# Query spread, maximum broadcast and row split in a cached-attention kernel

## The chip, the core and the metric

The kernel runs on one core of a Trainium2 chip. A core has TensorE (PE in the profile), VectorE (DVE), ScalarE (ACT), GpSimd (POOL) and SyncE (SP), which work side by side and wait for each other with semaphores, an on-chip memory of 128 partitions (SBUF), an accumulator memory that TensorE writes (PSUM), and 16 DMA engines that bring data from HBM. The metric is the device time of one execution in microseconds; the median of three runs is given.

## The reference

One decoding step of a block in which attention over a cache and a gated feed-forward network are mixed by a gate. There are 4 batches, 32 heads, 4096 cached positions and 128 numbers a head, all float32:

```python
q = (x @ wq).reshape(B, 1, 32, 128)            # x: (4, 1, 512)
scores = einsum("bhqd,bhkd->bhqk", q, k_cache) * 128 ** -0.5
p = softmax(scores)
a = (p @ v_cache).reshape(B, 1, 4096) @ wo
b = (gelu(x @ w_gate) * (x @ w_up)) @ w_down   # 512 -> 1792 -> 512
g = sigmoid((x * gate_w).sum(-1, keepdims=True))
return g * a + (1 - g) * b
```

The two caches are 268 MB each, and every number of them is used once. wq and wo are 8.4 MB each, the three FFN weights 3.7 MB each.

## The kernel before, in words

**Tiles and loads.** A tile is one batch and two heads (HT = 2); there are NT = 64 tiles, and four tiles (one pair of heads, all batches) form a group g. Partition p of a tile belongs to head p // 64 and holds R = 64 positions of 128 numbers, so K and V of a tile are 4 MB each, 32 KB a partition. All big loads share a ring of NB = 5 buffers of that size (pool kv) and are issued in one order by SyncE: two of wq, k0, k1, v0, k2, v1 and so on, the gate and up weights behind v19 and v20 (FFN_AT = 20), k62 and k63 together ahead of v61, and w_down last, in four transfers of which the last is half as big. V of tile 63 comes in two halves. A load is issued when the buffer five loads earlier in that order is free. wo comes in eight transfers of 1 MB in a buffer of its own, one for two groups.

**Scores.** VectorE multiplies K by the query, which has to stand on all partitions of its head (`QB[g]`, made by `q_spread`), and sums each row of 128. `MOST` splits the 64 rows of a tile for the first 62 tiles: three pieces "D" of 20 rows that VectorE both multiplies and sums, and one piece "A" of 4 rows whose products ScalarE sums, with one activation a row (`sums`, L201 to L207). `LAST` splits the last two tiles (NL = 2), in which ScalarE sums 24 of the 64 rows; "U" is a second such piece in a buffer u of its own.

**Softmax.** `max_a` takes the maximum of each partition and transposes it to one row in PSUM. `soft_max` reduces that row to a maximum for each head (m2), sends it to the 64 partitions of its head with two small matmuls against ones (L233), scales it on ScalarE (nb) and takes two exponentials, whose sums are the denominators. The result lands in PM, in columns so that a matmul of 32 columns puts each head and batch in a row of its own.

**P times V and after.** `pv` accumulates 16 matmuls a tile over a group in PO; the profile lists two records for each of them. `gather` adds the four position classes of a group to 8 rows of 128 numbers (batch and head) and the denominators. `weigh` divides (ri, on) and, for each head and each of four 32-number pieces, multiplies by a column pattern `hsel` that repeats each batch eight times and picks the head: 8 matmuls a group, which put the transposed result in OT. `project_a` copies OT and multiplies by wo, 16 matmuls for two groups, into a_acc.

**Order.** Every engine runs its instructions in the order in which the program issues them. In tile i: the first product of tile i, then `soft_max(i - 1)`, in every fourth tile `weigh`, then the other products and sums of tile i, `pv(i - 1)`, `max_a(i)`, in some tiles `project_a`, the next `load_wo` and `q_spread` of the next group. After the loop stand pv of the last tile, the four parts of `ffn_down` (each waits for its transfer of w_down), and between them gather, weigh and project_a of the last group; then ta, res and the store.

Of the kernel before, what the change touches and what calls it, by code (L numbers as in the profile page):

```python
# [9 lines left out]
F32 = mybir.dt.float32  # L10
AF = mybir.ActivationFunctionType
OP = mybir.AluOpType
AX = mybir.AxisListType
# [4 lines left out]
def tile_gated_mix(ctx: ExitStack, tc: tile.TileContext, x, kc, vc, wq, wo, w_gate, w_up, w_down, gate_w, out):  # L18
    nc = tc.nc
    P = 128  # L20
    B, H, S, D = kc.shape
    DM = x.shape[2]
    F = w_gate.shape[1]
    KC = DM // P
    C4 = DM // 4
    HT = 2
    PH = P // HT
# [3 lines left out]
    TW = R * D  # L31
    RJ = 4

    MOST = (("A", 60, 64), ("D", 0, 20), ("D", 20, 40), ("D", 40, 60))
    LAST = (("U", 48, 56), ("A", 60, 64), ("D", 0, 20), ("U", 40, 48), ("A", 56, 60), ("D", 20, 40))
    NL = 2
    FFN_AT = 20
# [4 lines left out]
    consts = ctx.enter_context(tc.tile_pool(name="consts", bufs=1))  # L42
    kv = ctx.enter_context(tc.tile_pool(name="kv", bufs=NB))
    work = ctx.enter_context(tc.tile_pool(name="work", bufs=2))
# [35 lines left out]
    def load_next():  # L80
        n = next(loads, None)
        if n:
            load(*n)
# [5 lines left out]
        nc.sync.dma_start(WO[w], wo[w * 4 * D:(w + 1) * 4 * D, :].rearrange("(p e) n -> p e n", e=4))  # L89

    load_next()
    x_sb = consts.tile([B, DM], F32)
    nc.sync.dma_start(x_sb, x.rearrange("b s d -> (b s) d"))
    load_next()
    for _ in range(NB - 2):
# [4 lines left out]
    ident = consts.tile([P, P], F32)  # L100
    make_identity(nc, ident)
    ones = consts.tile([P, P], F32)
# [3 lines left out]
    for j in range(RJ):  # L106
        nc.vector.tensor_reduce(sel[:, j], ident.rearrange("p (c b m) -> p b m c", c=4, b=B)[:, :, HT * j:HT * (j + 1), :],
                                axis=AX.X, op=OP.add)

    hsel = consts.tile([B * HT, HT, B, 8], F32)  # L110
    for h in range(HT):
        nc.vector.tensor_copy(hsel[:, h], ident[:B * HT, h:B * HT:HT][:, :, None].to_broadcast([B * HT, B, 8]))


    PZ = 32 - RJ * HT
# [32 lines left out]
    for c in range(KC):  # L148
        w = T["q", c // 2].rearrange("p (c n) -> p c n", c=2)[:, c % 2, :]
# [7 lines left out]
    QT = consts.tile([P, 4, HG, B], F32)  # L157
    for s in range(2):
        ps = ps1.tile([P, HB, P], F32, name="q")
# [5 lines left out]
    QT = QT.rearrange("p j a b -> p (j a) b")  # L165
# [5 lines left out]

    def q_spread(g):
        ps = ps1.tile([P, B, D], F32, name="q")
        for b in range(B):
            for h in range(HT):
                nc.tensor.matmul(ps[h * PH:(h + 1) * PH, b, :], QT[:, HT * g + h, b:b + 1].to_broadcast([P, PH]),  # L176
                                 ident, start=True, stop=True)
        QB[g] = work.tile([P, B, D], F32, name="qb")
        nc.scalar.activation(QB[g], ps, AF.Copy)  # L179

# [5 lines left out]
    def parts(i):  # L186
        return LAST if i >= NT - NL else MOST

# [38 lines left out]
    def soft_max(i):  # L227
        g, b = divmod(i, B)
        m2 = work.tile([1, HT], F32, name="m2")
        nc.vector.tensor_reduce(m2, MT[i].rearrange("o (h p) -> o h p", h=HT), axis=AX.X, op=OP.max)  # L230
        nbp = ps2.tile([P, 1], F32, name="sm")
        for h in range(HT):
            nc.tensor.matmul(nbp[h * PH:(h + 1) * PH, :], ones[:1, :PH], m2[:, h:h + 1], start=True, stop=True)  # L233
        nb = work.tile([P, 1], F32, name="nb")
        nc.scalar.activation(nb, nbp, AF.Copy, scale=-scale)  # L235
        for h in range(HT):
            s = slice(h * PH, (h + 1) * PH)
            nc.scalar.activation(PM[i % 2][:, PZ:].rearrange("p (c m) -> p c m", m=32)[s, :, h:RJ * HT:HT],  # L238
                                 SC[i][s, :].rearrange("p (c j) -> p c j", j=RJ), AF.Exp, bias=nb[s, :], scale=scale,
                                 accum_out=RS[g % 2][s, b, h:h + 1])  # L240
# [6 lines left out]
    def project(acc, t, w, start, stop):  # L247
        for c in range(4):
            nc.tensor.matmul(acc[32 * c:32 * c + 32, :], t, w[:, c * C4:(c + 1) * C4], start=start, stop=stop)  # L249
# [11 lines left out]
    OS, OT = {}, {}  # L261
# [8 lines left out]
        nc.tensor.matmul(OS[g][:, D:], RS[g % 2].rearrange("p b h -> p (b h)"), ones[:, :1], start=True, stop=True)  # L270


    def weigh(g):
        ri = work.tile([B * HT, 1], F32, name="ri")
        nc.vector.reciprocal(ri, OS[g][:, D:])
        on = work.tile([B * HT, 4, D // 4], F32, name="on")
        nc.vector.tensor_scalar(on, OS[g][:, :D].rearrange("p (k e) -> p e k", e=4), ri, None, op0=OP.mult)  # L277
        w, r = divmod(g, 2)
        if r == 0:
            OT[w] = ps1.tile([P, 4, 32], F32, name="oT")  # L280
        for h in range(HT):
            q = 32 * (HT * r + h)
            for e in range(4):
                nc.tensor.matmul(OT[w][q:q + 32, e, :], on[:, e, :], hsel[:, h].rearrange("p b k -> p (b k)"),
                                 start=True, stop=True)

    def project_a(w):
        ot = work.tile([P, 4, 32], F32, name="ot")
        nc.scalar.activation(ot, OT[w], AF.Copy)
        for e in range(4):  # L290
            project(a_acc, ot[:, e, :], WO[w][:, e, :], (w, e) == (0, 0), (w, e) == (H // 4 - 1, 3))
# [34 lines left out]
    def ffn_down(j):  # L326
        w = T["d", 0].rearrange("p (f n) -> p f n", n=DM)
        for f in range(j * FG // P, min((j + 1) * FG, F) // P):
            project(b_acc, hT[:, f, :], w[:, f, :], f == 0, f == F // P - 1)


    q_spread(0)
    for i in range(NT):
        g, b = divmod(i, B)
        pair = i > B and i % B == 1
        first = scores_a(i)
        if 0 < i < NT - 1:
            soft_max(i - 1)
        if pair:
            weigh(g - 1)  # L340
        scores(i, first)
        load_next()
        if i == NT - 2:
            max_a(i)
            soft_max(i)
        if i == NT - 1:
            pv(i - 1, 0, 4)
            max_a(i)
            pv(i - 1, 4, 8)
            soft_max(i)  # L350
            pv(i - 1, 8)
        elif i > 0:
            pv(i - 1)
            load_next()
            if b == 0:
                gather(g - 1)
# [10 lines left out]
        if i + B < NT and b == 1:  # L367
            q_spread(g + 1)
# [7 lines left out]
    gather(H // HT - 1)  # L376
    ffn_down(1)
    weigh(H // HT - 1)
    ffn_down(2)
    project_a(H // 4 - 1)  # L380
    ta = consts.tile([P, C4], F32)
    nc.vector.tensor_scalar(ta, a_acc, g_cols[:, 0:1], None, op0=OP.mult)
    ffn_down(3)
    res = work.tile([P, C4], F32, name="res")
    nc.vector.scalar_tensor_tensor(res, b_acc, g_cols[:, 1:2], ta, op0=OP.mult, op1=OP.add)
    nc.sync.dma_start(out.rearrange("b s (c n) -> c (b s) n", c=4), res[::8])

# [21 lines left out]
```

## Time and profile before

| | us |
|---|---|
| median of 3 runs (1323.89 to 1324.14) | 1323.95 |
| the profiled execution | 1324.15 |
| its span, first to last instruction | 1322.4 |
| VectorE busy | 1157.2 |
| TensorE busy (matmuls) | 498.6 |
| ScalarE busy | 210.4 |
| GpSimd busy | 0.7 |

The page gives, in turn: the busy time of each engine; the span in 40 slices with the busy share of each engine in tenths, the share of time in which the DMA engines move data and their rate; the DMA queues; the chain of work that ended last, by engine; the costliest groups of instructions (line, engine, operation, out<-in, shape, count, then total busy us and mean ns, then the engine's idle time just before them and what ended most of it); and the transfers with the median time from issue to landing. A view of windows gives the busy time of PE, PE's weight loads, VectorE, ScalarE and GpSimd in a stretch, then the granted TensorE clock, the DMA share and GB/s. A timeline row is the start in us, the duration, engine, line, operation, and in brackets the idle time before it with its releaser. Matmul times are modelled, and the granted clock was 0.659 on average here.

### The profile page before, as it was taken

To read this page: it belongs to the slowest core of one execution; us is meant where nothing else is said; L and a number is where in the kernel's file an instruction comes from. 1 tells how busy PE (TensorE), PEld (TensorE's weight loads), DVE (VectorE), ACT (ScalarE), POOL (GpSimd) and SP (SyncE) were. 2 spreads that over 40 slices of the span, in tenths; PEclk is the share of its full clock that TensorE was granted. 3 is DMA by queue.
4 is the path that set the end of the run, shared out by engine and by line. 5 is a ranking of instruction groups with operands and counts; after the bars stand their busy time and mean duration, and the time that the engine had idled before them with its cause. 6 is when DMAs were issued, how large, how long until landed. Compare 5 with 4: busy or idle time off the path is not lost.

```text
span 1322.4 us, 9351 instructions
## 1 busy us (share of the span) xinstructions
PE 498.6 (38%) x3562; PEld 177.8 (13%) x3562; DVE 1157.2 (88%) x645; ACT 210.4 (16%) x963; POOL 0.7 (0%) x6
## 2 busy tenths in 40 slices
PE   3242433342442453433344243352433343253316
PEld 1011111111110110111111011110101111011102
DVE  1999899989899579998999989899899989999894
ACT  0111111101111111101101101101101101111133
POOL 0000000000000000000000000000000000000000
PEclk9566667666775775766766665766766665666668
DMA  9999999999999999999999999999999999999997
GB/s 411 430 427 429 434 433 431 428 429 433 432 432 429 430 433 431 431 427 433 431 434 432 429 432 431 431 430 431 433 429 431 431 434 431 428 431 430 436 430 315
DMA packets 21096, 565.28 MB, mean 427 GB/s; under 512 B 2472, under 2 KB 2488, under 8 KB 2620
## 3 DMA queue, kind: packets, MB, share of 16 engines
q1 hardware_dynamic: 21052, 564.69, 99.4%
q8 instruction: 28, 0.46, 0.1%
q14 instruction: 16, 0.13, 0.0%
HBM read 564.67 MB, written 0.01 MB: 427 GB/s over the span
## 4 chain that ended last, share of the span: by engine, by line
DMA 71%; DVE 24%; PE 4%; issue 0%; SPq 0%; ACT 0%; DVEq 0%
DMA kv<-in_A_k_cache 51%; DMA kv<-in_A_v_cache 18%; DVE pr L197 13%; DVE sc L204 9%; PE po L256 3%; DMA kv<-in_B_w_down 3%; DVE pa L197 1%; DVE m L230 0%; SPq L59 0%; DVE u L197 0%; PE sm L135 0%; PE b_acc L249 0%; PE q L322 0%; DVE m L223 0%; DVE on L277 0%
## 5 line engine op out<-in xcount | busy, mean ns | idle before, releaser
L256 PE MATMUL po<-kv,pm 128*32 128x512 f32 x2048 | 368.3, 884 | 493.9 <-DMA kv<-in_A_v_cache 488.4
L204 DVE TENSOR_REDUCE sc<-pr 128x20 f32<-128x2560 f32 x190 | 535.8, 2820 | 6.5
L197 DVE TENSOR_TENSOR pr<-kv,qb 128x2560 f32<-128x2560 f32 x190 | 535.3, 2817 | 4.2
L256 PEld LDWEIGHTS po<-kv,pm 128*32 128x32 f32 x2048 | 91.7, 155 | 715.4 <-issue 704.2
L197 DVE TENSOR_TENSOR pa<-kv,qb 128x512 f32<-128x512 f32 x66 | 45.6, 690 | 90.9 <-DMA kv<-in_A_k_cache 90.9
L235 ACT ACTIVATE nb<-sm 128x1 f32<-128x1 f32 x64 | 10.9, 170 | 574.2 <-PE sm L233 574.1
L225 PE MATMUL sm<-ident,m 128*1 128x128 f32 x64 | 19.2, 299 | 199.3 <-DVE m L223 199.3
L207 ACT ACTIVATE dump<-pa 128x128 f32<-128x128 f32 x264 | 81.7, 309 | 10.5 <-DVE pa L197 2.6
L233 PE MATMUL sm<-m,ones 1*64 1x1 f32 x256 | 22.4, 238 | 88.6 <-DVE m L230 88.6
L179 ACT ACTIVATE qb<-q 128x512 f32<-128x512 f32 x16 | 9.6, 597 | 261.1 <-PE q L176 261.1
L207 ACT ACTIVATION_READ_ACCUMULATOR dump<-pa 128x1 f32 x264 | 49.2, 186 | 0.0
L238 ACT ACTIVATE pm<-sc,nb 64x64 f32<-64x64 f32 x128 | 44.6, 348 | 3.0 <-ACT nb L235 0.2
L265 ACT ACTIVATE o<-po 128x512 f32<-128x512 f32 x16 | 9.6, 597 | 194.0 <-PE po L256 194.0
L225 PEld LDWEIGHTS sm<-ident,m 128*1 128x1 f32 x64 | 5.1, 79 | 243.3 <-issue 211.1
L233 PEld LDWEIGHTS sm<-m,ones 1*64 1x64 f32 x256 | 17.0, 182 | 106.4 <-DVE m L230 98.9
L176 PE MATMUL q<-ident,QT 128*64 128x128 f32 x256 | 27.2, 381 | 0.6 <-DVE QT L163 0.6
L238 ACT ACTIVATION_READ_ACCUMULATOR pm<-sc,nb 64x1 f32 x128 | 23.6, 185 | 0.0
L176 PEld LDWEIGHTS q<-ident,QT 128*64 128x64 f32 x256 | 21.5, 194 | 4.4 <-issue 3.0
L268 PE MATMUL sm<-o,sel 128*8 128x128 f32 x128 | 16.6, 273 | 10.7 <-ACT o L265 10.7
L223 DVE TENSOR_REDUCE m<-sc 128x1 f32<-128x64 f32 x64 | 14.1, 220 | 6.6
L230 DVE TENSOR_REDUCE m<-sm 1x2 f32<-1x128 f32 x64 | 17.4, 272 | 1.1 <-PE sm L225 1.1
L268 PEld LDWEIGHTS sm<-o,sel 128*8 128x8 f32 x128 | 10.3, 89 | 26.8 <-ACT o L265 24.9
(56 smaller groups left out, 129.3 us busy)
## 6 DMA issues: line engine op xcount, KB each, us to landing
kv<-in_A_k_cache SPq DMA_DIRECT2D x64, 4096.0 KB, 42.6
kv<-in_A_v_cache SPq DMA_DIRECT2D x63, 4096.0 KB, 34.0
kv<-in_A_wq SPq DMA_DIRECT2D x2, 4096.0 KB, 16.6
wo_sb<-in_A_wo SPq DMA_DIRECT2D x8, 1024.0 KB, 40.7
kv<-in_A_v_cache SPq DMA_DIRECT2D x2, 2048.0 KB, 39.7
kv<-in_B_w_gate SPq DMA_DIRECT2D x1, 3584.0 KB, 44.1
kv<-in_B_w_up SPq DMA_DIRECT2D x1, 3584.0 KB
kv<-in_B_w_down SPq DMA_DIRECT2D x3, 1024.0 KB, 30.4
```

The source lines that it names most:

```text
L176: nc.tensor.matmul(ps[h * PH:(h + 1) * PH, b, :], QT[:, HT * g + h, b:b + 1].to_broadcast([P, PH]), ident, start=True, stop=True)
L197: nc.vector.tensor_tensor(t, T["k", i].rearrange("p (r d) -> p r d", d=D)[:, r0:r1], QB[g][:, b:b + 1, :].to_broadcast([P, n, D]), op=OP.mult)
L204: nc.vector.tensor_reduce(SC[i][:, r0:r1], t, axis=AX.X, op=OP.add)
L207: nc.scalar.activation(dump, t[:, r - r0, :], AF.Copy, accum_out=SC[i][:, r:r + 1])
L223: nc.vector.tensor_reduce(m1, SC[i], axis=AX.X, op=OP.max)
L225: nc.tensor.transpose(MT[i], m1, ident)
L230: nc.vector.tensor_reduce(m2, MT[i].rearrange("o (h p) -> o h p", h=HT), axis=AX.X, op=OP.max)
L233: nc.tensor.matmul(nbp[h * PH:(h + 1) * PH, :], ones[:1, :PH], m2[:, h:h + 1], start=True, stop=True)
L235: nc.scalar.activation(nb, nbp, AF.Copy, scale=-scale)
L238: nc.scalar.activation(PM[i % 2][:, PZ:].rearrange("p (c m) -> p c m", m=32)[s, :, h:RJ * HT:HT], SC[i][s, :].rearrange("p (c j) -> p c j" ...
L256: nc.tensor.matmul(PO[g % 2][32 * c:32 * c + 32].rearrange("p j d -> p (j d)"), PM[i % 2][:, m0:m0 + 32], T["v", i][:, j * N:(j + 1) * N], ...
L268: nc.tensor.matmul(OS[g][:, :D], sel[:, j].rearrange("p b h -> p (b h)"), o[:, j, :], start=j == 0, stop=j == RJ - 1)
```

## The change

Five things are changed. (1) `q_spread`: GpSimd copies the query columns of a group to qx, each number repeated over the 64 columns of its head, and TensorE transposes the four batches: 4 transposes instead of 8 matmuls against a broadcast operand. qx has one buffer, which x used at the start. (2) `soft_max`: GpSimd copies the two maxima to a row of 128 (mb), and one transpose puts it on the partitions, instead of two matmuls. (3) `weigh`: VectorE makes a version of the divided rows for each head, with zeros for the other, so that 4 matmuls of 64 columns do what 8 of 32 did; hsel becomes small and bsel is new. (4) `MOST`: VectorE multiplies and sums all 64 rows in three pieces of 22, 21 and 21; ScalarE's piece is left in the last two tiles only. (5) In the tail, `project_a` of the last groups is issued ahead of `ffn_down(2)` instead of behind it. The tiles on and res have one buffer instead of two.

```diff
--- before.py
+++ after.py
@@ -31,7 +31,7 @@
     TW = R * D
     RJ = 4
 
-    MOST = (("A", 60, 64), ("D", 0, 20), ("D", 20, 40), ("D", 40, 60))
+    MOST = (("D", 0, 22), ("D", 22, 43), ("D", 43, 64))
     LAST = (("U", 48, 56), ("A", 60, 64), ("D", 0, 20), ("U", 40, 48), ("A", 56, 60), ("D", 20, 40))
     NL = 2
     FFN_AT = 20
@@ -89,7 +89,7 @@
         nc.sync.dma_start(WO[w], wo[w * 4 * D:(w + 1) * 4 * D, :].rearrange("(p e) n -> p e n", e=4))
 
     load_next()
-    x_sb = consts.tile([B, DM], F32)
+    x_sb = work.tile([B, DM], F32, name="qx", bufs=1)
     nc.sync.dma_start(x_sb, x.rearrange("b s d -> (b s) d"))
     load_next()
     for _ in range(NB - 2):
@@ -107,9 +107,11 @@
         nc.vector.tensor_reduce(sel[:, j], ident.rearrange("p (c b m) -> p b m c", c=4, b=B)[:, :, HT * j:HT * (j + 1), :],
                                 axis=AX.X, op=OP.add)
 
-    hsel = consts.tile([B * HT, HT, B, 8], F32)
-    for h in range(HT):
-        nc.vector.tensor_copy(hsel[:, h], ident[:B * HT, h:B * HT:HT][:, :, None].to_broadcast([B * HT, B, 8]))
+    hsel = consts.tile([B * HT, HT], F32)
+    nc.vector.tensor_reduce(hsel, ident[:B * HT, :B * HT].rearrange("p (b h) -> p h b", h=HT), axis=AX.X, op=OP.add)
+    bsel = consts.tile([B * HT, B, 8], F32)
+    nc.vector.tensor_copy(bsel, ident[:B * HT, 0:B * HT:HT][:, :, None].to_broadcast([B * HT, B, 8]))
+    nc.vector.tensor_tensor(bsel, bsel, ident[:B * HT, 1:B * HT:HT][:, :, None].to_broadcast([B * HT, B, 8]), op=OP.add)
 
 
     PZ = 32 - RJ * HT
@@ -171,10 +173,11 @@
 
     def q_spread(g):
         ps = ps1.tile([P, B, D], F32, name="q")
+        qx = work.tile([P, B, HT, PH], F32, name="qx", bufs=1)
+        nc.gpsimd.tensor_copy(qx, QT[:, HT * g:HT * g + HT, :].rearrange("p h b -> p b h")[:, :, :, None]
+                              .to_broadcast([P, B, HT, PH]))
         for b in range(B):
-            for h in range(HT):
-                nc.tensor.matmul(ps[h * PH:(h + 1) * PH, b, :], QT[:, HT * g + h, b:b + 1].to_broadcast([P, PH]),
-                                 ident, start=True, stop=True)
+            nc.tensor.transpose(ps[:, b, :], qx[:, b].rearrange("p h k -> p (h k)"), ident)
         QB[g] = work.tile([P, B, D], F32, name="qb")
         nc.scalar.activation(QB[g], ps, AF.Copy)
 
@@ -228,9 +231,10 @@
         g, b = divmod(i, B)
         m2 = work.tile([1, HT], F32, name="m2")
         nc.vector.tensor_reduce(m2, MT[i].rearrange("o (h p) -> o h p", h=HT), axis=AX.X, op=OP.max)
+        mb = work.tile([1, HT, PH], F32, name="mb", bufs=1)
+        nc.gpsimd.tensor_copy(mb, m2[:, :, None].to_broadcast([1, HT, PH]))
         nbp = ps2.tile([P, 1], F32, name="sm")
-        for h in range(HT):
-            nc.tensor.matmul(nbp[h * PH:(h + 1) * PH, :], ones[:1, :PH], m2[:, h:h + 1], start=True, stop=True)
+        nc.tensor.transpose(nbp, mb.rearrange("o h k -> o (h k)"), ident[:1, :1])
         nb = work.tile([P, 1], F32, name="nb")
         nc.scalar.activation(nb, nbp, AF.Copy, scale=-scale)
         for h in range(HT):
@@ -270,19 +274,22 @@
         nc.tensor.matmul(OS[g][:, D:], RS[g % 2].rearrange("p b h -> p (b h)"), ones[:, :1], start=True, stop=True)
 
 
+
     def weigh(g):
         ri = work.tile([B * HT, 1], F32, name="ri")
         nc.vector.reciprocal(ri, OS[g][:, D:])
-        on = work.tile([B * HT, 4, D // 4], F32, name="on")
-        nc.vector.tensor_scalar(on, OS[g][:, :D].rearrange("p (k e) -> p e k", e=4), ri, None, op0=OP.mult)
+        rh = work.tile([B * HT, HT], F32, name="rh")
+        nc.vector.tensor_scalar(rh, hsel, ri, None, op0=OP.mult)
+        on = work.tile([B * HT, 4, HT, D // 4], F32, name="on", bufs=1)
+        for h in range(HT):
+            nc.vector.tensor_scalar(on[:, :, h, :], OS[g][:, :D].rearrange("p (k e) -> p e k", e=4), rh[:, h:h + 1], None,
+                                    op0=OP.mult)
         w, r = divmod(g, 2)
         if r == 0:
             OT[w] = ps1.tile([P, 4, 32], F32, name="oT")
-        for h in range(HT):
-            q = 32 * (HT * r + h)
-            for e in range(4):
-                nc.tensor.matmul(OT[w][q:q + 32, e, :], on[:, e, :], hsel[:, h].rearrange("p b k -> p (b k)"),
-                                 start=True, stop=True)
+        for e in range(4):
+            nc.tensor.matmul(OT[w][64 * r:64 * r + 64, e, :], on[:, e].rearrange("p h k -> p (h k)"),
+                             bsel.rearrange("p b k -> p (b k)"), start=True, stop=True)
 
     def project_a(w):
         ot = work.tile([P, 4, 32], F32, name="ot")
@@ -376,12 +383,12 @@
     gather(H // HT - 1)
     ffn_down(1)
     weigh(H // HT - 1)
+    project_a(H // 4 - 1)
     ffn_down(2)
-    project_a(H // 4 - 1)
     ta = consts.tile([P, C4], F32)
     nc.vector.tensor_scalar(ta, a_acc, g_cols[:, 0:1], None, op0=OP.mult)
     ffn_down(3)
-    res = work.tile([P, C4], F32, name="res")
+    res = work.tile([P, C4], F32, name="res", bufs=1)
     nc.vector.scalar_tensor_tensor(res, b_acc, g_cols[:, 1:2], ta, op0=OP.mult, op1=OP.add)
     nc.sync.dma_start(out.rearrange("b s (c n) -> c (b s) n", c=4), res[::8])
```

## The prediction

> **What bounds the kernel now.** I read the page first: the busy sums, the tenths, the DMA queues and the chain that ended last.
>
> ```profile
> PE 498.6 (38%) x3562; PEld 177.8 (13%) x3562; DVE 1157.2 (88%) x645; ACT 210.4 (16%) x963; POOL 0.7 (0%) x6
> DMA  9999999999999999999999999999999999999997
> GB/s 411 430 427 429 434 433 431 428 429 433 432 432 429 430 433 431 431 427 433 431 434 432 429 432 431 431 430 431 433 429 431 431 434 431 428 431 430 436 430 315
> q8 instruction: 28, 0.46, 0.1%
> q14 instruction: 16, 0.13, 0.0%
> DMA 71%; DVE 24%; PE 4%; issue 0%; SPq 0%; ACT 0%; DVEq 0%
> kv<-in_A_k_cache SPq DMA_DIRECT2D x64, 4096.0 KB, 42.6
> kv<-in_A_v_cache SPq DMA_DIRECT2D x63, 4096.0 KB, 34.0
> ```
>
> The 16 DMA engines are full from the first slice to the last but one, at 427 to 436 GB/s. DVE's 88% is the tempting wrong reading, so I asked what DVE waits for, and then cut the span into stages.
>
> ```profile
> L197 DVE TENSOR_TENSOR pa<-kv,qb 128x512 f32<-128x512 f32 x66 | 45.6, 690 | 90.9 <-DMA kv<-in_A_k_cache 90.9
> L256 PE MATMUL po<-kv,pm 128*32 128x512 f32 x2048 | 368.3, 884 | 493.9 <-DMA kv<-in_A_v_cache 488.4 <-ACT dump L207 2.9 <-ACT pm L238 2.6
> 34.00:1300.00 1266.00, 470.51 (x3239) 165.83 (x3239) 1149.43 (x615) 204.61 (x949) 0.00 (x0) 0.65 1.00 431
> 1310.00:1315.00 5.00, 3.98 (x86) 2.63 (x78) 0.49 (x2) 0.60 (x1) 0.00 (x0) 1.00 0.71 296
> 1315.00:1318.00 3.00, 2.11 (x76) 1.86 (x72) 0.00 (x0) 0.28 (x1) 0.00 (x0) 1.00 0.31 119
> ```
>
> Both consumers end their waits on a landing: the first product of a tile on K (90.9 us), P times V on V (488.4 us). In the last row's columns, DMA share and GB/s close each line: 1.00 and 431 over 1266 us. So one 4 MB transfer takes 4.194 MB / 431 GB/s = 9.73 us, and the kernel is 565 MB at that rate plus a head and a tail. Compute matters only if it empties the DMA queue or lengthens the tail.
>
> How far from empty is it? From issue to landing a K transfer takes 42.6 us and a V 34.0 us (medians), of which its own movement is 9.73: some 33 and 24 us of work stand ahead of each at its issue. The tightest stretch is the start, where DVE still works off its backlog:
>
> ```profile
> 32.49 0.69 DVE pa L197
> 101.82 0.33 SPq L59
> 102.25 40.94 DMA kv<-in_A_k_cache
> 143.20 0.69 DVE pa L197
> ```
>
> The K issued at 102.25 landed 40.94 later, so 31.2 us were ahead of it; the V issued just before, at 101.82, had 31.2 - 9.7 + 0.4 = 21.9 us ahead. That is the lead: a buffer must come free some **20 us later** than now before the chip's DMA pauses.
>
> **The change, part by part.**
>
> *All 64 rows on VectorE.* Gone are one product of 4 rows and ScalarE's 4 sums a tile; the three pairs grow from 20 to 22, 21 and 21 rows.
>
> ```profile
> L204 DVE TENSOR_REDUCE sc<-pr 128x20 f32<-128x2560 f32 x190 | 535.8, 2820 | 6.5
> L197 DVE TENSOR_TENSOR pr<-kv,qb 128x2560 f32<-128x2560 f32 x190 | 535.3, 2817 | 4.2
> L223 DVE TENSOR_REDUCE m<-sc 128x1 f32<-128x64 f32 x64 | 14.1, 220 | 6.6
> L230 DVE TENSOR_REDUCE m<-sm 1x2 f32<-1x128 f32 x64 | 17.4, 272 | 1.1 <-PE sm L225 1.1
> L277 DVE TENSOR_SCALAR on<-sm,ri 8x128 f32<-8x128 f32 x16 | 5.4, 339 | 0.6
> ```
>
> Products of 512 and 2560 elements (690 and 2817 ns) give (2817 - 690) / 2048 = 1.04 ns an element and 0.16 us fixed. So 22 rows take 3.08 us and 21 rows 2.95; a tile's products and sums go from 3 x (2.82 + 2.82) + 0.69 = 17.60 to 2 x (3.08 + 2.95 + 2.95) = 17.97 us. With both maxima (0.22 + 0.27) that is 18.09 before and 18.46 after. weigh() adds one tiny multiply (about 0.15, as other tiny ones) and a second 0.34 per four tiles: from 0.12 to 0.24 us a tile, so 18.70 in all. The DMA period of a tile is 2 x 9.73 = 19.46, and with 1 MB of wo every eighth tile 19.77. VectorE stays **1.07 us a tile** inside it. Its total rises by 62 x 0.37 + 16 x 0.49 = 31 us to about 1188; cost 0. The cover is the landing wait of the pa row; were it gone, each tenth of a microsecond over would cost 62 x 0.1 = 6 us.
>
> In the backlog phase, six tiles from 32.49 to 143.20, K buffers come free up to 6 x 0.4 = 2.4 us later: 19.5 us of lead are left. The first product now takes 3.08 instead of 0.69, and the maximum of the tile before (L230) stands behind it, so softmax and P times V can start 2.4 us later. V lands 9.73 us after K, which hides it; where it doesn't, V buffers go back 2 to 3 us later, against more than 20. ScalarE loses 62 x 4 sums: it is at 16% and releases nothing on the chain, so nothing.
>
> *Maxima and queries through GpSimd.* No row shows such a copy. The nearest:
>
> ```profile
> masks.py:199 POOL TENSOR_SCALAR_AFFINE_SELECT ident<-ident 128x128 f32<-128x128 f32 x1 | 0.3, 292 | 0.1
> L398 POOL MEMSET const-float32-0.0<- 128x1 f32 x1 | 0.1, 98 | 0.2 <-issue 0.2
> 29.99 0.60 ACT L179 ACTIVATE qb<-q 128x512 f32<-128x512 f32 x1 [2.89 <-PE q L176]
> ```
>
> One element takes 98 ns, 128 take 292: 1.5 ns each. So mb (128 elements) takes 0.3 us and qx (512) 0.9; the low ends are 0.1, the high ends 5 us (held up behind three products, below). I take 0.3 and 0.9. In the loop both stand ahead of P times V and are hidden like the 2.4 us above. At the head, qb is ready at 30.59 and K lands at 32.49: 1.9 us of cover. Behind a late mb wait PE's next transpose, weigh's matmuls and P times V; then the V buffer, with its 20 us of lead.
>
> *TensorE.* A matmul has two records, a transpose one (L225: 64 transposes, 64 records).
>
> ```profile
> L176 PE MATMUL q<-ident,QT 128*64 128x128 f32 x256 | 27.2, 381 | 0.6 <-DVE QT L163 0.6
> L233 PE MATMUL sm<-m,ones 1*64 1x1 f32 x256 | 22.4, 238 | 88.6 <-DVE m L230 88.6
> L284 PE MATMUL oT<-hsel,on 8*32 8x32 f32 x256 | 11.4, 213 | 2.1 <-DVE on L277 1.7
> ```
>
> These become 64, 64 and 128 records: 512 fewer, and as many weight loads. Busy PE was never the bound: 0. But instructions are themselves fetched over the 16 engines (the two instruction queues, 0.59 MB). With 1024 fewer on PE, 496 on ACT, some 44 on DVE and 80 more on POOL, 16% of the 9351 go, about 0.09 MB. Spread evenly at 431 GB/s that is 0.2 us; all on the engine that ends last (431 / 16 = 27 GB/s), 3.5 us. The engines do end unevenly: the two tail windows leave 5 x 0.29 + 3 x 0.69 = 3.5 us idle on average before the last one is through. I take **-0.6**, nearer to the even share, and keep -0.2 to -3.5.
>
> *The tail.*
>
> ```profile
> 1314.13 1.08 PE L249 MATMUL b_acc<-kv,hT 128*32 128x128 f32 x32 [0.49 <-DMA kv<-in_B_w_down]
> 1315.76 0.28 ACT L289 ACTIVATE ot<-oT 128x128 f32<-128x128 f32 x1 [3.94 <-PE oT L284]
> 1316.62 1.08 PE L249 MATMUL b_acc<-kv,hT 128*32 128x128 f32 x32 [0.89 <-DMA kv<-in_B_w_down]
> 1317.51 1.06 PE L249 MATMUL a_acc<-wo_sb,ot 128*32 128x128 f32 x32
> 1318.39 0.62 PE L249 MATMUL b_acc<-kv,hT 128*32 128x128 f32 x16
> 1319.11 0.35 DVE L385 SCALAR_TENSOR_TENSOR res<-b_acc,g_cols,ta 128x128 f32<-128x128 f32 x1
> ```
>
> The second and third piece of w_down land 2.49 us apart (1314.13 and 1316.62); the fourth is half as big, so it is there at about 1317.87, while its matmuls start at 1318.39 because project_a stands before them. Moved ahead of ffn_down(2), project_a runs in the wait before 1316.62 (ot is ready at 1316.04), and the last matmuls start with their data: **-0.5** (0 if ot comes 0.5 us later; weigh's extra 0.5 us on DVE is hidden behind ffn_down(1)).
>
> Sum on the profiled execution (1324.15, span 1322.4, 1.75 around it): -0.6 - 0.5 = -1.1, 1323.05. That execution lies 0.2 above the median 1323.95, so the forecast is **1322.9**.
>
> **The rivals.** *A: the tail's GpSimd copies are locked out.* In the last two tiles the order after a maximum is product, product, product:
>
> ```profile
> 1286.01 0.28 DVE L230 TENSOR_REDUCE m<-sm 1x2 f32<-1x128 f32 x1 [0.56 <-PE sm L225]
> 1286.22 1.20 DVE L197 TENSOR_TENSOR u<-kv,qb 128x1024 f32<-128x1024 f32 x1
> 1287.95 2.80 DVE L197 TENSOR_TENSOR pr<-kv,qb 128x2560 f32<-128x2560 f32 x1
> 1293.53 1.21 DVE L197 TENSOR_TENSOR u<-kv,qb 128x1024 f32<-128x1024 f32 x1
> 1301.03 0.22 DVE L223 TENSOR_REDUCE m<-sc 128x1 f32<-128x64 f32 x1
> 1311.22 0.60 ACT L265 ACTIVATE o<-po 128x512 f32<-128x512 f32 x1 [6.14 <-PE po L256]
> ```
>
> If a copy can't read SBUF while DVE multiplies, mb waits from 1286.2 to 1290.8. ScalarE's exponentials and its 24 sums of tile 63 queue behind it, so u and pa are read 4.6 us later than now; the second u product, at 1293.53, has some 1.6 us to spare, and the maximum at 1301.03 comes about 3 us later. Tile 62 has the same order, so 6 us together: 1307. From there the path has softmax (3 us, copy included) and P times V (32 records of 0.11 to 0.21 us by the clock, 3.4 to 6.8 us), which ends at 1313.5 to 1317 instead of 1311.2. From that point to the end of res it is 8.3 us today (to 1319.46), 1.5 of them waits for w_down that would be gone: res ends at 1320.3 to 1323.8, against 1318.95 in the forecast. Price +1.4 to +4.8, so 1324.3 to 1327.7, middle 1326. Against it: one product may let the copy in (then 0). In all other tiles a sum of 3 us follows the maximum, and the copy fits beside it. The Trainium skill states such a lock (SBUF — State Buffer, Who interferes with whom): a VectorE instruction with two SBUF inputs and a GpSimd one that reads SBUF exclude each other for a whole instruction. No run here shows it yet.
>
> *B: transfers get slower by their place in SBUF.* x and hsel leave the constants (2048 + 96 bytes a partition, tiles rounded to 32), so all kv buffers move down by 2144 = 8 x 256 + 96 bytes. For: 1 MB of w_down, in rows a quarter as long, takes 2.49 us where 431 GB/s gives 2.43: 0.06 us for 6 more rows on each engine (128 rows over 16 engines make 8 a transfer, where 1 MB of K would have 2), 10 ns each, so a row has a fixed cost. With 8 rows an engine in 9.73 us that is 0.8% of the transfer, some 10 us of 1266; if a worse start adds between a quarter and all of it, 2.5 to 10 us, middle 6.3: 1329.2. Against: nothing in this trace varies the start. The Trainium skill (DMA: Bandwidth & Descriptors, How a descriptor splits into AXI transactions) lets a descriptor that starts off a 256-byte boundary pay for the bytes below its start; no run here shows that for a write.
>
> *C: VectorE becomes the bound.* If GpSimd's reads hold up products by 1.5 us a tile, 0.43 x 62 = 27 us less the 20 of lead: 1330. The copies last 0.3 us, so unlikely.
>
> *D: the fetches saved sit on the last engine.* -3.5 instead of -0.6: 1320.0. For: the 3.5 us of uneven end. Against: one engine would have to carry all of them.
>
> **How the numbers follow.** Forecast 0.66, A 0.13, B 0.08, C 0.05, D 0.08. A measurement here tells 0.2% from no change, 2.65 us: faster is under 1321.3, slower over 1326.6. Faster: most of D and 0.02 of the forecast's spread, 0.09. Slower: B, C and half of A, 0.20. Same: 0.71. The range 1320.5 to 1328.5 leaves out B, C, A's top and D's bottom, 0.18; the forecast's own range is 1321.5 to 1324.0.
>
> **What would show it.** Right: DMA share 1.00 and 431 GB/s over the middle, DVE busy near 1188 us with its idle time still ended by K landings, POOL copies near 0.3 and 0.9 us, issue-to-landing times within 3 us of 42.6 and 34.0, the last b_acc matmuls ended by w_down's landing, fewer instruction bytes. Wrong: under 429 GB/s in the middle (B), products that last over 3.1 us or idle time on GpSimd (C), or a tail in which the last maximum comes over 2 us later against the last landing (A).

## The result, and the profile after

| | us | runs |
|---|---|---|
| before | 1324.05 (1323.86 to 1324.16) | 11 |
| after | 1327.21 (1326.58 to 1328.34) | 11 |
| ratio after / before | 1.0024, 95% interval 1.0015 to 1.0034 | |

The change costs 3.2 us, just over the 2.65 us that the prediction called no change. The forecast of 1322.9 is missed by 4.3 us; the time lies inside the range, where rival A put it (1324.3 to 1327.7).

First the page of the changed kernel: busy sums, tenths of the DMA share, GB/s, the two instruction queues, the chain that ended last, and issue to landing.

```profile
PE 490.0 (37%) x3050; PEld 168.5 (13%) x3050; DVE 1195.6 (90%) x616; ACT 112.4 (8%) x467; POOL 35.3 (3%) x86
DMA  9999999999999999999999999999999999999996
GB/s 412 427 428 431 436 428 427 432 434 429 429 431 432 429 432 430 433 431 428 430 432 432 430 431 430 431 431 430 431 431 432 432 428 431 430 435 426 430 434 283
q8 instruction: 24, 0.39, 0.1%
q14 instruction: 13, 0.11, 0.0%
DMA 51%; DVE 37%; issue 6%; PE 4%; ACT 1%; POOL 1%; SPq 0%; DVEq 0%; ACTq 0%
kv<-in_A_k_cache SPq DMA_DIRECT2D x64, 4096.0 KB, 41.8
kv<-in_A_v_cache SPq DMA_DIRECT2D x63, 4096.0 KB, 33.7
```

From the view of windows, the middle of the span (stretch, its length, busy time of PE, PE's loads, VectorE, ScalarE, GpSimd, then clock, DMA share, GB/s):

```profile
34.00:1300.00 1266.00, 462.91 (x2742) 157.04 (x2742) 1181.71 (x581) 102.33 (x431) 33.67 (x78) 0.65 1.00 431
```

The middle is as it was: a DMA share of 1.00 and 431 GB/s, as before, and a K still lands 41.8 us after its issue and a V 33.7 (42.6 and 34.0 before), so the queue did not run dry. 0.50 MB of instructions are fetched instead of 0.59. Of the slices only the last moved clearly fewer GB/s, 283 instead of 315; the others differ by a few GB/s either way. That points at the tail, behind the stream. The chain has shifted from DMA (71% to 51%) to VectorE (24% to 37%), but this says nothing of the tail: in e1 below, where the tail is on time again, the chain has 53% and 37%, and in e13, with the row split alone, 64% and 32%.

So I looked at the tail's timeline of the changed kernel, GpSimd first (start, duration, engine, line, operation, idle time before it and its releaser):

```profile
1271.40 3.42 POOL L235 COPY mb<-m 1x128 f32<-1x128 f32 x1 [17.30 <-DVE m L233]
1289.06 4.56 POOL L235 COPY mb<-m 1x128 f32<-1x128 f32 x1 [14.24 <-DVE m L233]
1307.87 0.28 POOL L235 COPY mb<-m 1x128 f32<-1x128 f32 x1 [14.25 <-DVE m L233]
```

The same copy of 128 numbers takes 0.28 us after the last maximum, and 3.42 and 4.56 us in the two tiles before. VectorE over the second of them, in the same timeline:

```profile
1288.93 1.20 DVE L200 TENSOR_TENSOR u<-kv,qb 128x1024 f32<-128x1024 f32 x1
1290.06 0.67 DVE L200 TENSOR_TENSOR pa<-kv,qb 128x512 f32<-128x512 f32 x1
1290.66 2.81 DVE L200 TENSOR_TENSOR pr<-kv,qb 128x2560 f32<-128x2560 f32 x1
1293.51 2.82 DVE L207 TENSOR_REDUCE sc<-pr 128x20 f32<-128x2560 f32 x1
1298.56 1.23 DVE L200 TENSOR_TENSOR u<-kv,qb 128x1024 f32<-128x1024 f32 x1 [2.24 <-ACT dump L210]
1300.30 0.69 DVE L200 TENSOR_TENSOR pa<-kv,qb 128x512 f32<-128x512 f32 x1 [0.51 <-ACT dump L210]
1306.69 0.22 DVE L226 TENSOR_REDUCE m<-sc 128x1 f32<-128x64 f32 x1
1322.16 0.35 DVE L392 SCALAR_TENSOR_TENSOR res<-b_acc,g_cols,ta 128x128 f32<-128x128 f32 x1 [0.96 <-PE b_acc L253]
```

The copy starts at 1289.06, 0.13 us after the first product has begun, and ends at 1293.62, when the last of the three products has ended (1290.66 + 2.81 = 1293.47) and the sum of L207 has begun. ScalarE's exponentials and sums wait for it; the next product into u then waits 2.24 us for ScalarE and the one into pa another 0.51. One tile earlier the picture is the same with two products (3.42 us) and waits of 2.17 and 0.51. Together that is 5.4 us, and the last maximum comes at 1306.69 instead of 1301.03.

### The profile page after: what moved, and what is told of

It is laid out like the page before. It is cut to its first block, busy times and chain, and to the rows that moved or that the text cites. A ratio compares the mean times of both kernels' runs of the same rounds, so it can differ in the third digit from the quotient of the medians.

```text
span 1325.4 us, 7916 instructions
## 1 busy us (share of the span) xinstructions
PE 490.0 (37%) x3050; PEld 168.5 (13%) x3050; DVE 1195.6 (90%) x616; ACT 112.4 (8%) x467; POOL 35.3 (3%) x86
## 4 chain that ended last, share of the span: by engine, by line
DMA 51%; DVE 37%; issue 6%; PE 4%; ACT 1%; POOL 1%; SPq 0%; DVEq 0%; ACTq 0%
DMA kv<-in_A_k_cache 41%; DVE sc L207 19%; DVE pr L200 16%; DMA kv<-in_A_v_cache 10%; PE po L260 3%; ACT dump L210 1%; DVE rh L282 1%; POOL mb L235 1%; DVE on L285 1%; DVE m L233 0%; PE q L310 0%; DVE m L226 0%; SPq L59 0%; PE b_acc L253 0%; ACT pm L242 0%
## 5 line engine op out<-in xcount | busy, mean ns | idle before, releaser
L200 DVE TENSOR_TENSOR pr<-kv,qb 128x2816 f32<-128x2816 f32 (+1 forms) x190 | 569.4, 2997 | 64.8 <-DMA kv<-in_A_k_cache 60.5
L207 DVE TENSOR_REDUCE sc<-pr 128x22 f32<-128x2816 f32 (+1 forms) x190 | 567.7, 2988 | 4.5
L237 PE MATMUL sm<-ident,mb 1*128 1x1 f32 x64 | 16.6, 259 | 222.7 <-POOL mb L235 222.7
L235 POOL COPY mb<-m 1x128 f32<-1x128 f32 x64 | 25.6, 400 | 1246.3 <-DVE m L233 1246.3
L237 PEld LDWEIGHTS sm<-ident,mb 1*128 1x128 f32 x64 | 11.2, 175 | 242.5 <-POOL mb L235 240.9
L291 PE MATMUL oT<-bsel,on 8*64 8x32 f32 x128 | 16.5, 287 | 13.9 <-DVE on L285 13.9
L180 PE MATMUL q<-ident,qx 128*128 128x128 f32 x64 | 16.8, 415 | 0.6 <-DVE QT L165 0.6
L291 PEld LDWEIGHTS oT<-bsel,on 8*64 8x64 f32 x128 | 14.4, 211 | 15.5 <-DVE on L285 15.5
L253 PE MATMUL a_acc<-wo_sb,ot 128*32 128x128 f32 x256 | 14.6, 401 | 0.4 <-ACT ot L296 0.4
## 6 DMA issues: line engine op xcount, KB each, us to landing
kv<-in_A_k_cache SPq DMA_DIRECT2D x64, 4096.0 KB, 41.8
kv<-in_A_v_cache SPq DMA_DIRECT2D x63, 4096.0 KB, 33.7
```

The lines of the kernel that those rows point to most:

```text
L180: nc.tensor.transpose(ps[:, b, :], qx[:, b].rearrange("p h k -> p (h k)"), ident)
L200: nc.vector.tensor_tensor(t, T["k", i].rearrange("p (r d) -> p r d", d=D)[:, r0:r1], QB[g][:, b:b + 1, :].to_broadcast([P, n, D]), op=OP.mult)
L207: nc.vector.tensor_reduce(SC[i][:, r0:r1], t, axis=AX.X, op=OP.add)
L235: nc.gpsimd.tensor_copy(mb, m2[:, :, None].to_broadcast([1, HT, PH]))
L237: nc.tensor.transpose(nbp, mb.rearrange("o h k -> o (h k)"), ident[:1, :1])
L291: nc.tensor.matmul(OT[w][64 * r:64 * r + 64, e, :], on[:, e].rearrange("p h k -> p (h k)"), bsel.rearrange("p b k -> p (b k)"), start=True ...
```

## The experiments

Twelve kernels, in three batches; the kernel before ran beside each batch (medians 1324.12, 1324.13 and 1324.08). The theory was that GpSimd's copies in the last tiles are locked out by VectorE's products (rival A); against it stood the new place of the kv buffers in SBUF (rival B), the new split of rows, and the new order at the end. Starts in SBUF are given modulo 256 bytes, from the allocation of each built kernel: kv begins at 64 in the kernel before and at 224 in the changed one.

### The tail's copies: one part out, one part alone

e1 is the changed kernel, in which only the last three softmaxes get their maxima by the two matmuls again:

```diff
         nbp = ps2.tile([P, 1], F32, name="sm")
+        if i >= NT - NL - 1:
+            for h in range(HT):
+                nc.tensor.matmul(nbp[h * PH:(h + 1) * PH, :], ones[:1, :PH], m2[:, h:h + 1], start=True, stop=True)
+        else:
+            mb = work.tile([1, HT, PH], F32, name="mb", bufs=1)
...
```

> The changed kernel, but the maxima of the last three tiles (61, 62, 63) go out by the two matmuls of before; GpSimd copies them in the first 61 tiles only. Theory: the 3.2 us lost are the two copies of 3.42 and 4.56 us that GpSimd could not start beside VectorE's products in the last two tiles; without them the last maximum comes at about 1301 instead of 1306.7 and the time is 1323 to 1324.3. Rival 'slower transfers' (another place in SBUF): nothing of that is changed, so 1327. Rival 'row split' (VectorE late at the end of the loop): 1327. Rival 'order of project_a': 1326.5 or more.

Measured: 1324.52 us (1324.22 to 1325.12), ratio to before 1.0004 (0.9995 to 1.0012). That is 0.2 above the expected range; e7 below shows what the place in SBUF has in it. In its timeline the last maximum and the last VectorE instruction (res) stand at

```profile
1300.92 0.22 DVE L226 TENSOR_REDUCE m<-sc 128x1 f32<-128x64 f32 x1
1319.38 0.35 DVE L396 SCALAR_TENSOR_TENSOR res<-b_acc,g_cols,ta 128x128 f32<-128x128 f32 x1 [0.96 <-PE b_acc L257]
```

The maximum is 5.8 us earlier than in the changed kernel, the end 2.8. The last three of the 64 copies, two of them held up, hold 2.7 us of the 3.2. (Their transposes went out with them; e5 below keeps all transposes and is as fast.)

e2 turns it round: the kernel before, with copy and transpose in the last three softmaxes alone (the condition is `if i < NT - NL - 1` for the matmuls).

> The kernel before, in which alone the maxima of the last three tiles go out by GpSimd's copy and one transpose. Theory: two copies of over 3 us, last maximum 5 to 6 us later, 1326 to 1327.5. Rivals (transfers, row split, order of project_a): all of them are as before, so 1324.1.

Measured: 1326.77 us (1326.52 to 1327.61), ratio 1.002 (1.0012 to 1.0029): 2.65 us slower. Its timeline shows the same lock and the same lateness:

```profile
1271.28 3.42 POOL L237 COPY mb<-m 1x128 f32<-1x128 f32 x1 [1269.98 <-DVE m L230]
1288.87 4.56 POOL L237 COPY mb<-m 1x128 f32<-1x128 f32 x1 [14.17 <-DVE m L230]
1306.49 0.22 DVE L223 TENSOR_REDUCE m<-sc 128x1 f32<-128x64 f32 x1
```

So the tail's copies cost about the same without any of the other edits, and most of the change's loss is in them.

### Is it GpSimd's read that is locked?

e5 keeps GpSimd's step, its place and its wait, but GpSimd only writes: it fills mb with zeros. The scores are then not reduced by their maximum before the exponential.

```diff
         mb = work.tile([1, HT, PH], F32, name="mb", bufs=1)
-        nc.gpsimd.tensor_copy(mb, m2[:, :, None].to_broadcast([1, HT, PH]))
+        nc.vector.tensor_reduce(mb[:, 0, :HT], MT[i].rearrange("o (h p) -> o h p", h=HT), axis=AX.X, op=OP.max)
+        nc.gpsimd.memset(mb, 0.0)
```

> The changed kernel, in which GpSimd does not copy the maxima but fills mb with zeros, at the same place in its order (VectorE's maximum is written into mb first, so that the fill waits for it): exponentials are taken without the maximum. The fill only writes. Theory in its strict form (a GpSimd instruction that reads SBUF is shut out by VectorE's products, one that only writes is not): the last fills take 0.1 to 0.3 us and the time is that of e1, 1324.5. Rival 'GpSimd starts late for another reason, any instruction of its own would' : fills of 3.4 and 4.6 us, 1327.2.

Measured: 1324.56 us (1324.2 to 1325.13), ratio 1.0003 (0.9994 to 1.0012), as e1. From its timeline, GpSimd beside VectorE:

```profile
1286.22 1.20 DVE L200 TENSOR_TENSOR u<-kv,qb 128x1024 f32<-128x1024 f32 x1
1286.35 0.20 POOL L234 MEMSET mb<- 1x128 f32 x1 [14.61 <-DVE mb L233]
1287.35 0.67 DVE L200 TENSOR_TENSOR pa<-kv,qb 128x512 f32<-128x512 f32 x1
1301.04 0.22 DVE L226 TENSOR_REDUCE m<-sc 128x1 f32<-128x64 f32 x1
```

The fill takes 0.20 us beside the first of the three products that held the copy for 4.56. What is shut out is GpSimd's read of SBUF, not its start and not its write. The Trainium skill says the same (SBUF — State Buffer, Who interferes with whom): a VectorE instruction with two inputs in SBUF shuts out a GpSimd one that reads SBUF, not one that only writes; e5 agrees, with 0.20 us.

### The rows, and the lock in all tiles

e4 is the changed kernel with the old `MOST`, so that a product (L200) follows the maximum instead of a sum, but for every fourth tile, where weigh stands between:

```diff
-    MOST = (("D", 0, 22), ("D", 22, 43), ("D", 43, 64))
+    MOST = (("A", 60, 64), ("D", 0, 20), ("D", 20, 40), ("D", 40, 60))
```

> The changed kernel with the old split of the rows (60 on VectorE, 4 on ScalarE) in the first 62 tiles. Behind each maximum VectorE then runs a product of 20 rows at once, not a sum. Theory: the copies of nearly all tiles last about 3 us instead of 0.28, yet the time stays at 1327 since V lands later than that; the tail is the same. Rival 'row split': back to 1324. Rival 'the lock costs in every tile': above 1328.

Measured: 1328.8 us (1327.57 to 1329.05, two groups near 1327.6 and 1328.9), ratio 1.0032 (1.0021 to 1.0044). From its timeline in mid-kernel, and then its page:

```profile
656.31 2.80 DVE L200 TENSOR_TENSOR pr<-kv,qb 128x2560 f32<-128x2560 f32 x1
656.44 2.82 POOL L235 COPY mb<-m 1x128 f32<-1x128 f32 x1 [16.37 <-DVE m L233]
659.15 2.82 DVE L207 TENSOR_REDUCE sc<-pr 128x20 f32<-128x2560 f32 x1
```

```profile
L235 POOL COPY mb<-m 1x128 f32<-1x128 f32 x64 | 139.8, 2184 | 1132.9 <-DVE m L233 1103.4
```

The copy now waits behind one product in most tiles: 45 of the 64 last 2.8 us and 17 still 0.28, 2184 ns on average over all. The 45 waits would be 114 us if they were on the path. The median is 1.6 us above the changed kernel's, where the rival 'the lock costs in every tile' was expected (above 1328) and not the theory (1327); but the intervals of the two kernels overlap, and the kept trace is of a run of the lower group. So a late copy in the middle, where the DMA queue has an estimated 20 us of lead, is hidden almost wholly or wholly, and the same lateness in the last two tiles is not. What the 1.6 us are was not settled.

e13 is the other half: the kernel before with the new `MOST` and nothing else.

> The kernel before with the new split of the rows alone (22, 21 and 21 on VectorE, none on ScalarE in the first 62 tiles); K and V buffers stay where they were. Theory and my prediction: hidden behind the landings, 1323.9 to 1324.2. Rival 'VectorE becomes late': above 1325.

Measured: 1324.16 us (1323.92 to 1325.71), ratio 1.0003 (0.9995 to 1.0012). From its page and its groups:

```profile
PE 499.9 (38%) x3562; PEld 179.1 (14%) x3562; DVE 1180.5 (89%) x583; ACT 112.3 (8%) x467; POOL 0.7 (0%) x6
```

```profile
L197 DVE TENSOR_TENSOR pr<-kv,qb 128x2816 f32<-128x2816 f32 (+1 forms) x190 | 569.7, 2998 | 76.7 <-DMA kv<-in_A_k_cache 72.4
```

VectorE does 23.3 us more and still ends its waits on K: the row split is free.

### The order at the end

e3 is the changed kernel with `project_a` behind `ffn_down(2)` again.

> The changed kernel with project_a again behind ffn_down(2). Theory: with the tail late, all of w_down has landed and TensorE is the bound after the last P times V; ffn_down(2) then fills the wait for ot (0.4 to 0.8 us), so 1326.4 to 1326.8, 0.4 to 0.8 below the changed kernel. Rival 'the order is the cause of the loss': 1324. My prediction's step (the new order gains 0.5 us): 1327.7.

Measured: 1327.31 us (1326.83 to 1327.91), ratio 1.0023 (1.0014 to 1.0032): 0.1 from the changed kernel, so neither the gain of 0.4 to 0.8 us that was expected for it is there nor the loss of 0.5 that followed from the prediction. From the changed kernel's timeline, and then from that of e3:

```profile
1309.41 6.35 PE L260 MATMUL po<-kv,pm 128*32 128x512 f32 x48
1315.84 0.60 ACT L269 ACTIVATE o<-po 128x512 f32<-128x512 f32 x1 [5.23 <-PE po L260]
1319.70 1.08 PE L253 MATMUL a_acc<-wo_sb,ot 128*32 128x128 f32 x32 [0.37 <-ACT ot L296]
```

```profile
1319.45 1.08 PE L253 MATMUL b_acc<-kv,hT 128*32 128x128 f32 x32
1320.35 1.06 PE L253 MATMUL a_acc<-wo_sb,ot 128*32 128x128 f32 x32
```

P times V ends so late that b_acc waits for w_down no longer: in e3 its third piece starts without a wait, where the kernel before waited 0.89 us for it. There is no wait left for project_a to fill. To see the order's worth with the tail on time, e7 and e8 start from e1 and put kv back at 64 with a constant of 96 bytes; e8 has the old order as well.

```diff
+    pad = consts.tile([P, 24], F32, name="pad")
+    nc.vector.memset(pad, 0.0)
```

> e1 with 96 bytes more among the constants, so that the K and V buffers stand at the same remainder of 256 bytes as in the kernel before (64 instead of 224). In e1 the tail's copies are gone and it is still at 1324.5, 0.4 above the kernel before, though fewer instructions are fetched. Theory 'place': the remaining 0.4 and the gains that did not show are transfers slower by 0.07%; then 1323.5 to 1323.8. Rival (the transfers' place does not matter; something else in the loop is slower): 1324.5.

> e7 (matmuls for the maxima of the tail, buffers at 64 of 256 bytes) with project_a behind ffn_down(2) again. Theory: with the tail on time the new order gains what I predicted or a little less, so this run is 0.3 to 0.5 above e7's 1323.34: 1323.6 to 1323.9. Rival (the order is worth nothing): 1323.3.

Measured: e7 1323.34 us (1323.13 to 1323.8), ratio 0.9995 (0.9986 to 1.0003); e8 1323.69 (1323.62 to 1324.06), ratio 0.9997 (0.9988 to 1.0006); e7 is 0.2 under its range, e8 as expected. By the medians the order is worth 0.35 us when the tail is on time. That is weakly shown: the ranges overlap, and in the two kept traces, both of runs above their medians, res starts only 0.07 us apart (1318.74 and 1318.81), since in e8's ot comes no earlier than the third piece of w_down (1316.35 and 1316.32). e7 against e1 gives the place: 1.2 us for 224 instead of 64.

### The place in SBUF alone

e9 and e10 are the kernel before with a constant that nothing reads, 160 or 192 bytes a partition, which puts kv at 224 or at 0 (e9 is shown; e10 has 48 in place of 40). The buffers of the pool behind kv, wo's and the queries' among them, move to the same remainder.

```diff
+    pad = consts.tile([P, 40], F32, name="pad")
+    nc.vector.memset(pad, 0.0)
```

> The kernel before with 160 bytes more among the constants: K and V buffers at 224 of 256 bytes instead of 64, as in the changed kernel; nothing else. Theory 'place': 1324.9 to 1325.1. Rival: 1324.1. My prediction's rival B in its own size: 1326.5 to 1334.

> The kernel before with 192 bytes more among the constants: K and V buffers start on a multiple of 256 bytes. Theory 'place' with a cost that falls with the remainder: 1323.6 to 1324.0. Rival (no matter): 1324.1.

Measured: e9 1325.3 us (1325.2 to 1326.99), ratio 1.001 (1.0001 to 1.0019), so 1.2 us slower than at 64, 0.2 more than expected; e10 **1318.94** (1318.78 to 1320.52), ratio 0.9964 (0.995 to 0.9977), 5.2 us faster. The sign was foreseen, the size of e10 was not. The middle of the span and two landings of w_down, in e9 by the views of windows and timeline (windows: stretch, its length, busy time of PE, PE's loads, VectorE, ScalarE, GpSimd, then clock, DMA share, GB/s):

```profile
34.00:1300.00 1266.00, 469.18 (x3231) 165.01 (x3231) 1148.52 (x615) 203.71 (x945) 0.00 (x0) 0.65 1.00 430
```

```profile
1315.18 1.08 PE L251 MATMUL b_acc<-kv,hT 128*32 128x128 f32 x32 [0.53 <-DMA kv<-in_B_w_down]
1317.67 1.08 PE L251 MATMUL b_acc<-kv,hT 128*32 128x128 f32 x32 [0.89 <-DMA kv<-in_B_w_down]
```

and in e10:

```profile
34.00:1300.00 1266.00, 473.86 (x3260) 165.71 (x3264) 1150.70 (x617) 205.53 (x953) 0.00 (x0) 0.65 1.00 432
```

```profile
1308.75 1.08 PE L251 MATMUL b_acc<-kv,hT 128*32 128x128 f32 x32 [0.46 <-DMA kv<-in_B_w_down]
1311.18 1.08 PE L251 MATMUL b_acc<-kv,hT 128*32 128x128 f32 x32 [0.83 <-DMA kv<-in_B_w_down]
```

The DMA share is 1.00 in both; the same engines move 432 instead of 430 GB/s, and the whole tail comes 6.4 us earlier (1308.75 against 1315.18). Two pieces of w_down land 2.43 us apart instead of 2.49.

### Both together

e12 is the changed kernel with 32 bytes more of constants (`[P, 8]`), kv at 0; e11 is that with e1's tail.

> The changed kernel with 32 bytes more among the constants: K and V buffers on a multiple of 256 bytes, the GpSimd copies of the tail left in. Theory: the transfers gain some 6 us against 224 (e9 less e10 gave 6.4), the tail's loss stays and hangs on the landing of the last K: 1320.8 to 1321.5. Rival (the late tail swallows the gain, since TensorE is the bound there): 1324 or more.

> e1 with 32 bytes more among the constants: no GpSimd copy in the tail, K and V buffers on a multiple of 256 bytes. Theory: e10's 1318.94 less the 0.75 that e7 gained on the kernel before: 1318.0 to 1318.5, below both kernels. Rival (the place is worth less here): 1320 or more.

Measured: e12 1321.49 us (1320.55 to 1322.3), ratio 0.9981 (0.9972 to 0.999); e11 **1317.90** (1317.72 to 1318.4), ratio 0.9954 (0.9941 to 0.9966), the first as expected, the second 0.1 under its range. From e11's windows and timeline:

```profile
34.00:1300.00 1266.00, 471.12 (x2789) 158.60 (x2793) 1188.21 (x586) 108.41 (x461) 25.61 (x76) 0.64 1.00 433
```

```profile
1311.15 1.49 PE L259 MATMUL b_acc<-kv,hT 128*32 128x128 f32 x48
1312.71 0.35 DVE L398 SCALAR_TENSOR_TENSOR res<-b_acc,g_cols,ta 128x128 f32<-128x128 f32 x1 [0.96 <-PE b_acc L259]
```

e11 beats both kernels: 6.2 us under the kernel before, 9.3 under the changed one. 32 bytes of constants bring 5.7 us with the locked tail and 6.6 without it.

### The sum

From the kernel before to the changed one, each term from a pair of runs: 1324.1; place 64 to 224, +1.2 (e9 against before); what is left when place, order and tail are as before, -0.4 (e8 against before, an interval that includes 0); the order with the tail on time, -0.35 (e7 against e8). That makes 1324.5, and e1 measured 1324.52. Then the locked copies of the last tiles: the changed kernel against e1 gives +2.7, which closes the sum by its making. e2 gives the same step independently: +2.65, and the order's 0.35 given back (e3), make 1327.5, measured 1327.21. The sum closes to 0.3 us. The query spread, the new weigh and the fetched instructions were never taken alone; they are inside the -0.4.

## Why the prediction was wrong, and where it was right

**The step that failed: the price of the copies in the last two tiles, which the sum put at nothing.** It took a copy at 0.3 us and as hidden. The mechanism by which it is not was written down and worked out as rival A, and then weighed at 0.13 on one sentence: "one product may let the copy in". No row stood behind that sentence, and the runs refute it. In e4 the copy waits out the one product beside it (2.82 us), and in the changed kernel it gets in neither beside nor between two and three products (3.42 and 4.56 us); it ends only when a sum has begun. These waits cost 2.7 us. The other 1.6 of the 4.3 us by which the forecast missed are the place in SBUF (+1.2, at nothing in the forecast) and two gains that came out smaller (below). The rest of rival A held: it put the last maximum at about 1307 (measured 1306.69), the end of P times V at 1313.5 to 1317 (o starts at 1315.84), the end of res at 1320.3 to 1323.8 (1322.16 + 0.35 = 1322.51), and the price at +1.4 to +4.8 (2.7). Its sign, a last maximum over 2 us later, is there with 5.7. The Trainium skill's rule (SBUF — State Buffer, Who interferes with whom), that the two exclude each other for a whole instruction, was cited beside it and given too little weight; the trace bears it out with those three durations.

**The place (rival B): the right thing, misread.** The 0.06 us by which w_down's pieces lag behind 431 GB/s were taken as a fixed cost of 10 ns a row, of which a worse start would add a quarter or more. A cost of about that size is there: single 8 KB packets of w_down last 313 to 315 ns on average at 64, so four of them last 35 to 41 ns longer than one of 32 KB (1218.5 ns), 12 to 14 ns for each of the three rows more; at 0 they last 309 to 310 ns, which leaves 7 to 9 ns a row. What failed is the step from it to the start: a 32 KB packet gets only 0.9 ns longer from 64 to 224, and the move adds 1.2 us, not 2.5 to 10. The kernel before was already paying; the 5 to 6 us lie in the move to 0, which the change did not make.

**The order: -0.5 forecast.** It is worth -0.35 by the medians with the tail on time, weakly shown, and nothing in the changed kernel. The step named the wait that it fills (the third piece of w_down), and this wait is just what a late tail takes away.

**Fetched instructions: -0.6 forecast.** 0.09 MB fewer are fetched, as predicted; the time left for it is the 0.4 us of e8 by the medians, in an interval that includes 0 and together with the parts that no run took alone. Rival D, in which one engine carries them all (-3.5), did not come about.

**What held.** The row split costs nothing (e13). DMA share 1.00 and an unchanged middle; the lead of 20 us was enough, and in e4 nearly or wholly enough for 2.8 us of lateness in most tiles. The small copy took 0.28 us where no product ran beside it (0.3 taken) and the large one 0.605 (0.9 taken). From the groups of the changed kernel:

```profile
L177 POOL COPY qx<-QT 128x512 f32<-128x512 f32 x16 | 9.7, 605 | 26.0 <-DVE QT L165 26.0
L282 DVE TENSOR_SCALAR rh<-hsel,ri 8x2 f32<-8x2 f32 x16 | 11.9, 743 | 0.6
```

VectorE's busy sum is 1195.6, where 1188 was forecast, and the second row more than accounts for it: rh was taken at 0.15 us and lasts 743 ns on average, 16 x 0.59 = 9.5 us more. Its cover held: the DMA share stays 1.00. Rival C had no place: products last 2997 ns on average. Two slips had no effect: the first slice of the kernel before moves 411 GB/s, not 427 to 436, and VectorE has 29 instructions fewer, not 44.

## What to carry to other kernels

In these runs a small GpSimd copy that reads SBUF ran freely beside VectorE's sums and waited out every product in a row of them; look at what VectorE runs right behind the copy's input, first of all in the tail, where no queue hides the wait. When a rival has been worked out, its chance needs a row as much as its price: here one unproven "may let it in" decided the forecast. In a kernel that is bound by DMA the start of the large buffers in SBUF is worth trying early (a multiple of 256 bytes was the best of the three tried here), since every edit of a constant can move it.

## What the runs showed of the hardware

**A 256-byte start in SBUF is worth 0.4% to 0.5% of a stream of 32 KB rows.** kv at 0 instead of 64 gives 5.2 us (e10), instead of 224 5.7 (e12) and 6.6 (e11). Only these three starts were tried. Single 32 KB packets of the DMA queue last 1214.8 ns on average at 0, 1218.5 at 64 and 1219.4 at 224, within 0.2 ns in all runs of the same start; with 1032 of them on each engine (129 transfers of 4 MB, 8 each), that is 3.8 us from 64 to 0 and 0.9 from 64 to 224, most of the 5.2 and 1.2 measured. The Trainium skill (DMA: Bandwidth & Descriptors, How a descriptor splits into AXI transactions) has a descriptor that starts off a 256-byte boundary pay in beats of 32 bytes for those below its start; it speaks of bytes that are fetched, while here the start of the write was moved. By that count, as an estimate, the step from 64 to 224 would cost five beats and the one from 0 to 64 two; the runs agree on the sign and not on the proportion, 1.2 us against 5.2: at the two other starts tried, most of the cost comes with being off 0 at all.

**The lock works the other way too.** VectorE in the changed kernel, at the end of a group, and GpSimd in the same time (timeline):

```profile
205.57 0.81 DVE L282 TENSOR_SCALAR rh<-hsel,ri 8x2 f32<-8x2 f32 x1
...
205.52 0.28 POOL L235 COPY mb<-m 1x128 f32<-1x128 f32 x1 [18.12 <-DVE m L233]
205.76 0.60 POOL L177 COPY qx<-QT 128x512 f32<-128x512 f32 x1
...
1317.79 0.22 DVE L282 TENSOR_SCALAR rh<-hsel,ri 8x2 f32<-8x2 f32 x1
```

A multiply of 16 numbers, issued while mb is being copied, ends with qx (205.57 + 0.81 = 206.38, 205.76 + 0.60 = 206.36); in the tail, without a copy beside it, it takes 0.22 us. It reads hsel and ri, both in SBUF. In e5, where a fill of 0.19 us stands in the place of the first copy, it is shorter by as much and again ends with qx (205.18 + 0.72 = 205.90, 205.28 + 0.60 = 205.88):

```profile
205.18 0.72 DVE L281 TENSOR_SCALAR rh<-hsel,ri 8x2 f32<-8x2 f32 x1
205.28 0.60 POOL L177 COPY qx<-QT 128x512 f32<-128x512 f32 x1
```

That it is held by the copies is read from these times; no run took qx away.
